# A halo of 32 columns instead of 8 in the x tile of a fused attention, channel mix and MLP kernel

## Chip, cores and metric

One core of a Trainium2 chip runs the kernel. The metric is the time of one execution on the device in microseconds, the median of several runs; lower is better.

## What is computed

Three layers follow each other on a batch of 4 sequences of 3072 tokens with 256 features, in float32:

```python
scores = (1.0 / S) * np.matmul(z, z.transpose(0, 2, 1))        # z: (4, 3072, 64)
x = u * np.matmul(np.maximum(scores, 0.0) ** 2, v)             # attention, gated by u

x_prev = x shifted by one token, zeros first
xk = mu_k * x + (1.0 - mu_k) * x_prev
xr = mu_r * x + (1.0 - mu_r) * x_prev
k = np.maximum(xk @ w_k, 0.0)                                  # w_k: (256, 1024)
x = 1.0 / (1.0 + np.exp(-(xr @ w_r))) * (k * k @ w_v)          # w_v: (1024, 256)

r = np.maximum(x.reshape(B * S, 256) @ w_in, 0.0)              # w_in: (256, 2048)
out = r * r @ w_out                                            # w_out: (2048, 256)
```

## The kernel before

Features lie on the 128 partitions and tokens along the free dimension, in blocks of T = 512 tokens; there are 24 blocks, and two neighbours make a pair (12 pairs). Every float32 operand is split into a high part and a rest, and each product is three matmuls: high by high, high by the weights' rest, rest by high. All matmuls have 512 moving columns.

Three stages use TensorE one behind the other. **Attention** makes scores from zz, keeps their squares in ahi and alo, and multiplies with vhl (L459); its matmuls have 64 rows, and two of them run at a time in the two halves of the array. The **channel mix** begins with the first two blocks done plainly (the plain stage: operands in mixed and hhi and hlo, weights in wk, wr and wv), and then takes the other 11 pairs with Winograd's form of a 2 by 2 matrix product (the mixed stage, since the work of three units is woven into each other by a planner in mix_groups). The **second MLP** takes all 12 pairs, numbered 0 to 11, in the same form.

In the Winograd form a pair is worked off in groups: 4 groups a pair in the mixed stage, 8 in the second MLP. A group is 7 products (product, L871, three matmuls each) between which the 8 down projections of the group before it are woven (down2, L887 to L889, three matmuls each): p0, d0, p1, d1, ..., p6, d6, d7, so 45 matmuls. In the mixed stage groups 1 and 2 of a pair have two gate sums of six matmuls besides (L219): 57. TensorE works this order off as written. Group i of the second MLP takes its up weights from win[i // 2]; the down projection of group i takes its weights from wout[i // 2], and runs during group i + 1.

The moving operands of products are made from a pair's x tile, x2. `pair_tile` makes it with HALO columns in front of each of its two halves of features; the last of them holds the token before the pair (`load_pair`, `before_x` read from column HALO - 1, L733 loads and L740 reads), and `pair_x` is the view without the halo. VectorE forms differences in place and in d13 (L833 to L837), then the operands are split: in the mixed stage and for pair 0 of the second MLP into unit tiles (L90, L764: u0 to u6, and two more, units 7 and 8, in a tile called mixed), later into the tiles ops0 (even pairs) and ops1 (odd pairs), whose names in the trace are b and d. The results of a product are summed on VectorE (L903), and go through relu, square and split on ScalarE and VectorE into hhi and hlo (L908, L912, L90, L920), the moving operands of the down projections.

Where the tiles lie in a partition follows from the order in which pools are made, since each side is a stack. On the left side x2 is the last tile but a few of its pool, and all that is made after it lies behind it. In bytes, with the remainder by 256 in brackets:

| tile | place before | role |
|---|---|---|
| vhl | 26880 and up (0) | weights in attention |
| zz | 76544 and up (0) | weights and moving, attention |
| ahi, alo | 105216 to 137984 (0) | moving, attention |
| hhi, hlo | 39168 to 63744 (0) | moving, down projections |
| x2 | 63744 to 72000 (0) | source of the operands |
| sig0, sig1, d13 | 72000, 74048, 76096 (64) | gates, differences |
| win0, wout0, win1, wout1 | 80192, 94528, 102720, 117056 (64) | weights, second MLP |
| u0 to u6 | 125248 to 153920 (64) | moving, products |
| ops0 (b, d of even pairs), in the place of u0 to u6 from pair 1 on | 125248 to 153920 (64) | moving, products |
| ops1 (b, d of odd pairs), ws, wk, wv, wr, mixed | 155392 and up (0) | moving and weights |
| win2, wout2, win3, wout3 | 184064, 198400, 206592, 220928 (0) | weights, second MLP |

All blocks of weights within a tile step by 512 bytes, all moving operands by 2048.

Of the kernel before, what the change touches and what calls it, by code (L numbers as in the profile page):

```python
# [23 lines left out]
def tile_relu2_attention__rwkv_channel_mix__relu2_mlp(  # L24
# [691 lines left out]

    unit = {}

    HALO = 8

    def pair_tile(s):
        x2_raw[s] = hp.tile([P, ND, HALO + 2 * T], F32, tag="x2", name="x2")
        return x2_raw[s]

    def pair_x(s):
        return x2_raw[s][:, :, HALO:].rearrange("x c (b t) -> x c b t", b=2)

    def load_pair(s):
# [3 lines left out]
        if t0:  # L732
            nc.sync.dma_start(out=t[:, :, HALO - 1:], in_=src[:, :, t0 - 1:t0 + 2 * T])  # L733
        else:
            nc.vector.memset(t[:, :, HALO - 1:HALO], 0.0)
            nc.sync.dma_start(out=t[:, :, HALO:], in_=src[:, :, 0:2 * T])

    def before_x(s, b, c, m):
        t0 = HALO - 1 + b * T
        nc.scalar.activation(out=m, in_=x2_raw[s][:, c, t0:t0 + T], func=AF.Copy, scale=om[:, 0, c:c + 1])  # L740
# [822 lines left out]
```

## Time and profile before

| | |
|---|---|
| median of 3 runs | 2495.2 us (2493.74 to 2495.23) |
| the profiled execution | 2495.45 us |
| its span, first to last instruction | 2493.6 us |
| TensorE busy | 2483.6 us (100%) |
| VectorE busy | 2104.8 us (84%) |
| ScalarE busy | 1823.0 us (73%) |
| granted clock of TensorE | 1.000 |
| chain of work that ended last | TensorE 94% of the span |

The span holds the kernel's instructions; some 1.9 us of the execution lie around it. Busy times are unions of an engine's instructions. The ends of matmuls are modelled, and each is shown longer than the distance to the next one's start, so for TensorE the starts are to be read.

### The profile page before, as it was taken

The page shows a single profiled execution, that of the slowest core. Times are in us where ns is not written, and L with a number is a line of the kernel's source. Part 1 is how long each engine was busy: PE and PEld are TensorE (multiplying, and loading weights), DVE is VectorE, ACT ScalarE, POOL GpSimd, SP SyncE. Part 2 cuts the span into 40 slices and gives each one's busy share as a digit, 9 for nine tenths or more (in the row PEclk, how much of TensorE's full clock was granted, in tenths as well). Part 3 has the DMA queues.
Part 4 walks back from the last instruction along what each step waited for, and adds up shares of the span by engine and source line. Part 5 has one row for each costly group of instructions (what it writes and reads, how often), then busy time and mean ns, then how long its engine had stood idle before and what let it go on. Part 6 is the DMA issues. An engine that isn't in the chain of part 4 may idle for free.

```text
span 2493.6 us, 39375 instructions
## 1 busy us (share of the span) xinstructions
PE 2483.6 (100%) x14721; PEld 2057.5 (83%) x14721; DVE 2104.8 (84%) x3499; ACT 1823.0 (73%) x3240; POOL 0.7 (0%) x6
## 2 busy tenths in 40 slices
PE   9999999999999999999999999999999999999999
PEld 7888898889988998888888888888888888888887
DVE  8898999889899889999999988777777777777776
ACT  8867977887698668888888877666666666666665
POOL 0000000000000000000000000000000000000000
PEclk9999999999999999999999999999999999999999
DMA  6676777767767752232132120110011001100100
GB/s 208 191 222 184 217 197 197 206 197 204 216 178 208 200 164 93 72 106 81 65 113 85 51 73 30 34 34 18 17 34 34 18 18 34 34 17 18 34 17 17
DMA packets 309439, 257.92 MB, mean 103 GB/s; under 512 B 205312, under 2 KB 224768, under 8 KB 306176
## 3 DMA queue, kind: packets, MB, share of 16 engines
q1 hardware_dynamic: 307136, 254.89, 34.8%
q8 instruction: 115, 1.88, 0.3%
q10 hardware_dynamic: 2112, 0.52, 0.1%
q14 instruction: 76, 0.62, 0.1%
HBM read 149.45 MB, written 105.91 MB: 102 GB/s over the span
## 4 chain that ended last, share of the span: by engine, by line
PE 94%; ACT 3%; DVE 1%; issue 1%; DMA 0%; SPq 0%; DVEq 0%
PE v L459 27%; PE ups L871 27%; PE v L887 10%; PE v L889 10%; PE v L888 10%; PE sps L421 4%; PE ups L219 4%; ACT a L382 1%; ACT a L425 1%; DVE alo L435 0%; DVE turn L362 0%; ACT vhl L328 0%; DMA mixed<-turned 0%; PE v L240 0%; PE v L238 0%
## 5 line engine op out<-in xcount | busy, mean ns | idle before, releaser
L459 PE MATMUL v<-ahi,vhl 64*128 64x512 f32 x4592 | 675.8, 387 | 0.0
L459 PEld LDWEIGHTS v<-ahi,vhl 64*128 64x128 f32 x4592 | 487.8, 184 | 69.6 <-ACT rest L469 3.7
L908 ACT ACTIVATE s<-s 128x512 f32<-128x512 f32 x288 | 181.0, 629 | 342.1 <-DVE s L903 342.1
L459 PE MATMUL v<-alo,vhl 64*128 64x512 f32 x2296 | 418.0, 386 | 0.2 <-DVE alo L435 0.2
L887 PE MATMUL v<-hhi,wout 128*128 128x512 f32 x768 | 303.2, 395 | 0.0
L889 PE MATMUL v<-hlo,wout 128*128 128x512 f32 x768 | 302.3, 394 | 0.0
L888 PE MATMUL v<-hhi,wout 128*128 128x512 f32 x768 | 301.6, 393 | 0.0
L871 PE MATMUL ups<-d,win 128*128 128x512 f32 x1056 | 301.1, 393 | 0.0
L459 PEld LDWEIGHTS v<-alo,vhl 64*128 64x128 f32 x2296 | 261.7, 184 | 34.0 <-DVE alo L435 0.6
L920 DVE TENSOR_TENSOR hlo<-s,hhi 128x512 fp32r<-128x512 f32 x384 | 264.5, 689 | 14.5 <-ACT hhi L90 1.0
L903 DVE TENSOR_TENSOR s<-ups,su 128x512 f32<-128x512 f32 x192 | 131.8, 687 | 126.9 <-PE ups L871 126.9
L871 PEld LDWEIGHTS ups<-d,win 128*128 128x128 f32 x1056 | 198.2, 188 | 45.7
L912 ACT ACTIVATE s<-s 128x512 f32<-128x512 f32 x384 | 231.3, 628 | 6.1
L871 PE MATMUL ups<-b,win 128*128 128x512 f32 x792 | 225.9, 393 | 0.0
L435 DVE TENSOR_TENSOR alo<-a,ahi 128x512 fp32r<-128x512 f32 x334 | 219.6, 661 | 0.0
L425 ACT ACTIVATE a<-a 128x512 f32<-128x512 f32 x334 | 211.4, 633 | 10.3
L362 DVE STREAM_TRANSPOSE turn<-a 128x512 f32<-128x512 f32 x240 | 206.7, 861 | 13.2 <-ACT a L425 11.9
L382 ACT ACTIVATE a<-sps 128x512 f32<-128x512 f32 x335 | 197.7, 590 | 20.2 <-PE sps L421 15.3
L871 PEld LDWEIGHTS ups<-b,win 128*128 128x128 f32 x792 | 148.7, 188 | 34.2
L889 PEld LDWEIGHTS v<-hlo,wout 128*128 128x128 f32 x768 | 144.1, 188 | 34.4
L887 PEld LDWEIGHTS v<-hhi,wout 128*128 128x128 f32 x768 | 144.2, 188 | 33.5
L888 PEld LDWEIGHTS v<-hhi,wout 128*128 128x128 f32 x768 | 144.3, 188 | 33.4
(201 smaller groups left out, 4284.5 us busy)
## 6 DMA issues: line engine op xcount, KB each, us to landing
turned<-turn SPq DMA_DIRECT2D x60, 1024.0 KB, 5.0
mixed<-turned SPq DMA_DIRECT2D x220, 256.0 KB, 5.1
u<-in_u_dram SPq DMA_DIRECT2D x192, 64.0 KB, 3.6
xT<-uT SPq DMA_DIRECT2D x48, 256.0 KB, 2.3
x2d<-sig SPq DMA_DIRECT2D x48, 256.0 KB, 2.1
x<-x2d SPq DMA_DIRECT2D x12, 1024.0 KB, 4.8
out_dram<-y SPq DMA_DIRECT2D x94, 128.0 KB, 2.3
raw<-in_v_dram SPq DMA_DIRECT2D x23, 512.0 KB, 5.2
```

What stands on the lines that cost most here:

```text
L362: nc.vector.transpose(t[:, :, :, c, :], a.rearrange("x (m r q) -> x q m r" if s else "x (m q r) -> x q m r", m=G, q=R))
L382: nc.scalar.activation(out=a, in_=ps, func=AF.Relu, scale=1.0 / S)
L425: nc.scalar.activation(out=a, in_=a, func=AF.Square)
L435: finish(lambda: nc.vector.tensor_tensor(out=lo, in0=a, in1=hi, op=ALU.subtract))
L459: nc.tensor.matmul(acc[n, d][i], lhsT=vt[rows, k % 2, c, ds_], rhs=at[s][k // 2][rows], start=first and k == 0, stop=last and k == 2)
L871: nc.tensor.matmul(ps, lhsT=weight(g, h, w), rhs=ops[g[0], j][y], start=first and m == 0, stop=m == 2, skip_group_check=not first)
L887: nc.tensor.matmul(acc[p, b][d], lhsT=w[:, 0, c, ds_], rhs=hi, start=first, stop=False)
L888: nc.tensor.matmul(acc[p, b][d], lhsT=w[:, 1, c, ds_], rhs=hi, start=False, stop=False)
L889: nc.tensor.matmul(acc[p, b][d], lhsT=w[:, 0, c, ds_], rhs=lo, start=False, stop=last)
L908: nc.scalar.activation(out=tmp[g, c], in_=banks[g, 0] if c == "11" else tmp[g, c], func=AF.Relu, scale=1.0 if g[0] < NPAIR else HS)
L912: nc.scalar.activation(out=tmp[g, c], in_=tmp[g, c], func=AF.Square)
L920: nc.vector.tensor_tensor(out=lo, in0=tmp.pop((g, c)), in1=hi, op=ALU.subtract)
```

## The change

`HALO` becomes 32. Each half of x2 gets 24 more columns in front, 192 bytes a partition in all, and the tiles made behind it on the left side move by as much. The halo's last column still holds the token before the pair. `prep_x2` reads x12 and x21 through a view whose step is HALO + T, which becomes 544 columns; it names the same elements.

```diff
     unit = {}
 
-    HALO = 8
+    HALO = 32
 
     def pair_tile(s):
         x2_raw[s] = hp.tile([P, ND, HALO + 2 * T], F32, tag="x2", name="x2")
```

## Rows read from the trace of the kernel before

**Rows 1.** The page, part 1: engine, busy us, share of the span, instructions.

```profile
PE 2483.6 (100%) x14721; PEld 2057.5 (83%) x14721; DVE 2104.8 (84%) x3499; ACT 1823.0 (73%) x3240; POOL 0.7 (0%) x6
```

**Rows 2.** Waits of TensorE, whole span: total us, times, longest; first and last of five.

```profile
PE sps L421 <- ACT a L382: 1.3, 3, 0.5
...
PE v L459 <- DVE alo L435: 0.2, 1, 0.2
```

**Rows 3.** Plain, mixed, second MLP: length; busy us (instructions) PE PEld DVE ACT POOL; clock; DMA.

```profile
919.59:962.93 43.34, 43.34 (x192) 35.86 (x191) 39.43 (x71) 35.38 (x62) 0.00 (x0) 1.00 0.43 151
962.93:1482.19 519.26, 519.26 (x2245) 421.34 (x2244) 485.50 (x823) 432.14 (x777) 0.00 (x0) 1.00 0.23 79
1482.19:2486.85 1004.67, 1004.67 (x4344) 815.14 (x4342) 750.83 (x1210) 652.00 (x1164) 0.00 (x0) 1.00 0.09 26
```

**Rows 4.** TensorE in order of time: first products of groups in pairs 1, 2, 11.

```profile
1576.22 0.86 PE L871 MATMUL ups<-b,win 128*128 128x512 f32 x3
1586.72 0.86 PE L871 MATMUL ups<-b,win 128*128 128x512 f32 x3
...
1607.72 0.85 PE L871 MATMUL ups<-b,win 128*128 128x512 f32 x3
1618.17 0.86 PE L871 MATMUL ups<-b,win 128*128 128x512 f32 x3
1628.40 0.84 PE L871 MATMUL ups<-b,win 128*128 128x512 f32 x3
1638.60 0.84 PE L871 MATMUL ups<-b,win 128*128 128x512 f32 x3
1648.80 0.85 PE L871 MATMUL ups<-b,win 128*128 128x512 f32 x3
...
1711.46 0.85 PE L871 MATMUL ups<-b,win 128*128 128x512 f32 x3
1721.92 0.86 PE L871 MATMUL ups<-b,win 128*128 128x512 f32 x3
1732.39 0.86 PE L871 MATMUL ups<-b,win 128*128 128x512 f32 x3
...
2451.24 0.86 PE L871 MATMUL ups<-b,win 128*128 128x512 f32 x3
2461.47 0.84 PE L871 MATMUL ups<-b,win 128*128 128x512 f32 x3
```

**Rows 5.** The same view, consecutive matmuls: mixed stage, then group 7 of pair 1.

```profile
1067.71 0.86 PE L871 MATMUL ups<-u,wk 128*128 128x512 f32 x3
1068.40 0.40 PE L887 MATMUL v<-hhi,wv 128*128 128x512 f32 x1
1068.64 0.39 PE L888 MATMUL v<-hhi,wv 128*128 128x512 f32 x1
...
1069.10 0.40 PE L871 MATMUL ups<-u,wse 128*128 128x512 f32 x1
...
1639.96 0.84 PE L871 MATMUL ups<-d,win 128*128 128x512 f32 x3
```

**Rows 6.** Waits in the mixed stage (962.93 to 1482.19): total us, times, longest.

```profile
ACT st L908 <- PE ups L871: 30.6, 20, 2.9
...
DVE st L903 <- PE ups L871: 12.7, 28, 1.1
```

**Rows 7.** Groups by line and shape: busy us, mean ns; idle us before, releaser.

```profile
L740 ACT ACTIVATE st<-x,om 128x512 f32<-128x512 f32 x44 | 31.0, 716 | 0.2 <-DMA x<-xT 0.2
...
L764 DVE TENSOR_TENSOR u<-x,u 128x512 fp32r<-128x512 f32 x47 | 31.6, 682 | 0.4 <-ACT u L90 0.3
...
L764 DVE TENSOR_TENSOR mixed<-x,mixed 128x512 fp32r<-128x512 f32 x13 | 8.9, 682 | 0.0
```

**Rows 8.** The page, part 6: DMA issues, count, KB each, us to landing.

```profile
x<-x2d SPq DMA_DIRECT2D x12, 1024.0 KB, 4.8
```

**Rows 9.** A stretch of attention: length; PE busy us (instructions), clock, DMA.

```profile
500.00:600.00 100.00, 100.00 (x883) 1.00 0.66 194
```

## The prediction

> **What bounds the kernel now.** The page's first part comes first: TensorE is busy for 2483.6 of 2493.6 us [rows 1]. Busy time alone proves little, since the ends of matmuls are modelled, so the second view is who waited for whom on TensorE: five entries, 3.7 us together, the longest a wait of scores for ScalarE and the shortest 0.2 us [rows 2]. All of them are waits of attention or of the prologue. Behind attention TensorE waits for nothing that the view can show, so the end of the kernel is a number of matmuls times the distance from one start to the next. That distance is what has to be read.
>
> The third view is the table by stage [rows 3]. I cut it at matmul starts. The plain stage (all operands at multiples of 256 bytes) has 191 starts in 43.34 us: 226.9 ns each. The mixed stage has 44 groups, 22 of 45 and 22 of 57 matmuls, 2244 in all, in 519.26 us: 231.4 ns each. The second MLP has 96 groups of 45 and 24 closing matmuls; 4343 starts lie in 1004.67 us: 231.3 ns each. The granted clock is 1.00, the 2.4 GHz level, in all three. So from the first Winograd product on each matmul takes about 4.5 ns longer than in the plain stage, with the same 512 columns, the same type and no wait.
>
> The fourth view is the order of time on TensorE, at the first product of groups of the second MLP [rows 4]. Groups do the same 45 matmuls; they differ in where the operands lie. In pair 2, group 6 (first product at 1711.46) takes 10.46 us and group 7 10.47 us; the products' operands are in ops0, 64 bytes past a multiple of 256, the weights in win3, wout2 and wout3 at multiples. In pair 1, group 1 (1576.22 to 1586.72) takes 10.50 us with operands in ops1 at multiples, and weights in win0 and wout0 64 bytes past. Group 4 (1607.72) has aligned products, but projects group 3's hidden tiles down with wout1, 64 bytes past: 10.45 us. Groups 5, 6 and 7 are the only ones with every operand at a multiple of 256: 10.23, 10.20 and 10.20 us. Pair 11, the last, repeats it: its group 5 takes 10.23 us again. Groups 6 and 7 carry the same side work in pair 1 as in pair 2, so that isn't the difference: the addresses are. 10.20 us over 45 is 226.7 ns, the distance of the plain stage.
>
> The same view at a finer grain [rows 5] shows where it sits: in the mixed stage the step from the first L887 behind the products of u (u at +64, wk and wv at multiples) to L888 is 0.24 us, and six matmuls take 1069.10 - 1067.71 = 1.39 us; the first six of group 7 in pair 1, all aligned, take 1639.96 - 1638.60 = 1.36 [rows 4, 5].
>
> **The change part by part.** *What moves.* The x2 tile grows from 2 x 1032 x 4 = 8256 bytes a partition (32 x 256 + 64) to 2 x 1056 x 4 = 8448 (33 x 256). What stands behind it on the left side moves by 192 bytes, from +64 to +0: sig, d13, win0, wout0, win1, wout1, the units u0 to u6, and ops0. No instruction, order, wait or count changes; the side still ends (at 154112) before the right side's tiles (155392), and each moved tile still covers parts of the same tiles of attention, so the waits for their release are the same. Attention itself isn't touched.
>
> *Second MLP.* Every operand of every matmul then lies as in groups 5 to 7. 4343 starts at 226.7 ns are 984.6 us instead of 1004.67: **20.1 us less**.
>
> *Mixed stage.* The u operands move to the residue of the unit tiles 7 and 8 and of wk, wv, wr. I price it at the plain stage's 226.9 ns: 2244 x 226.9 = 509.2 us instead of 519.26: **10.1 us less**, as long as VectorE keeps up. It is busy for 485.50 of the 519.26 us [rows 3], 93%; of 509.2 it would be 95%. What hides it is its idle time, 33.8 us in this stage, of which its longest wait, for products, makes 12.7 us; ScalarE waits 30.6 us for products at one line [rows 6]. TensorE asks for 10.1 us of that. If the cover failed, TensorE would wait for the hidden tiles, and the most that can be given back is the 10.1 us. In the second MLP VectorE has 750.83 us of work in 984.6: no bound, and the groups at 10.20 us show it.
>
> *Engines.* VectorE and ScalarE read and write moved tiles too. VectorE's split of an operand takes 682 ns into u (at +64) and 682 ns into a unit at a multiple [rows 7]. I take nothing, from 1 ns less to 1 ns more an instruction by the rounding of these rows, all of it beside TensorE's work.
>
> *DMA.* 23 loads write x2, whose rows begin at +32 and +64 (x itself), afterwards at +128 and +0. Such a load takes 4.8 us [rows 8], and its first reader in the mixed stage, L740, waited 0.2 us for all of them together [rows 7]. A gain or a loss within it isn't seen by the end; with the cover gone, a load would cost its excess, tenths of a microsecond each, 23 times. I take nothing.
>
> *Tail.* What follows the last matmul is unchanged, and so is all ahead of the mixed stage.
>
> *Sum.* 2495.45 us of the profiled execution (span 2493.6 and 1.85 around it) less 20.1 and 10.1 is 2465.25; the median of the runs lies 0.25 lower: **2465.0 us**, 1.2% less. Next in line then is the distance of 226.7 ns itself, in every stage.
>
> **The rivals.** *A, slower: the residue that counts is of more than 256.* The tiles that are good today are all odd multiples of 256 (hi, lo, wv, win2, win3, ops1: remainder 256 by 512); the moved tiles become even multiples (win0 at 80384, remainder 0). If what matters is that moving operand and weights agree modulo 512 or more, the change only turns a difference of 64 into one of 256. Against it: within win and wout the blocks of weights step by 512 bytes, and groups 6 and 7 show no step. For it: no row of this trace has a difference of 256. It decides above 231.3 ns a matmul. With the dearest group of rows 4, 10.50 us or 233.3 ns for each of the 6587 starts, it would be 6587 x 2.0 = 13 us slower: 2508 us. Chance 0.07.
>
> *B, no change: not the address but the region or the company.* Today's slow operands all lie between 80192 and 153920, so "shifted" and "in the middle" are the same tiles. Against it: attention's ahi and alo are moving operands, and zz is both, at multiples of 256 in that same region, and a stretch of 100 us holds 883 half-array matmuls, one more or less at its edges, two of which run at a time [rows 9]: 100 / 441 = 226.8 ns for two, the good distance. For it: those are half-array matmuls of 64 rows. It gives 2495 us. The Trainium skill, in SBUF — State Buffer, section Specifications (TRN2), gives a cacheline of 16 bytes; +64 is a multiple of 16, and by that alone the two places would read equally fast and the time would stay at 2495 us. The trace disagrees with that reading: 10.20 against 10.46 us for the same group. Chance 0.05.
>
> *C, part is given back.* VectorE, with 5% of idle time left in the mixed stage, lets TensorE wait at some groups, or a few matmuls keep some ns: 2466 to 2490 us, about 2475 if the mixed stage gains nothing. For it: in that stage VectorE is the nearest engine; against: TensorE hasn't one wait there today. Chance 0.08.
>
> *The forecast*, 2465 us: 0.80.
>
> **How the numbers follow.** The forecast's own bounds: 0.2 ns a matmul either way is 1.3 us, a run-to-run spread of 1.5 us, and the mixed stage's 10.1 us as the price of lost cover on the upper side. Low 2461, high 2476: this holds the forecast nearly whole (0.78) and half of C (0.04). Faster by over 0.2%, 5 us, about what a measurement of this kernel can tell from no change: 0.80 + 0.08 = 0.88. Within: B, 0.05. Slower: A, 0.07.
>
> **What would show it.** Right, if in the profile after all groups of the second MLP take 10.20 us in even and odd pairs alike, the stage from the first product with win to the last matmul some 985 us, the mixed stage some 509, the plain stage 43.3 as now, and TensorE's waits behind attention stay empty. Even pairs at 10.46 would mean B; even pairs changed but not at 10.20, or odd groups 5 to 7 fast while 1 to 4 stay at 10.50, would mean A; entries "PE <- DVE" in the mixed stage would mean C. The forecast is wrong if the distance between matmul starts depends on something that the moved tiles share with their neighbours besides the last 8 bits of their address.

## The result and the profile after

The changed kernel takes 2464.0 us (2463.4 to 2465.6, 4 runs) against 2494.5 of the kernel before: a ratio of 0.988, 95% interval 0.986 to 0.990. The profiled execution took 2465.6 us, its span is 2463.8. The forecast was 2465.0, and its range 2461 to 2476 holds the time.

The table by stage of the changed kernel (plain, mixed, second MLP; length, busy us and instructions of PE, PEld, DVE, ACT, POOL, then clock, DMA share, GB/s). The second MLP is taken from the start of its first matmul to the start of its last:

```profile
920.64:963.98 43.34, 43.34 (x192) 35.85 (x191) 39.46 (x71) 35.40 (x62) 0.00 (x0) 1.00 0.43 151
963.98:1472.62 508.64, 508.64 (x2245) 421.17 (x2244) 484.81 (x823) 431.21 (x777) 0.00 (x0) 1.00 0.24 81
1472.62:2457.19 984.57, 984.57 (x4344) 814.90 (x4343) 749.51 (x1210) 652.16 (x1164) 0.00 (x0) 1.00 0.09 27
```

The row of the second MLP in [rows 3] ends at 2486.85, the start of the last matmul but one, so it holds 4342 starts and not 4343 (the count of instructions in a row takes in those that only reach into its stretch). Taken to the start of the last matmul, the kernel before has (length, busy us and instructions of PE, clock, DMA share, GB/s):

```profile
1482.19:2487.08 1004.89, 1004.89 (x4344) 1.00 0.09 26
```

The plain stage is what it was, 43.34 us. The mixed stage lost 519.26 - 508.64 = 10.6 us, the second MLP 1004.89 - 984.57 = 20.3. Both now run at 226.7 ns a matmul (508.64 / 2244, 984.57 / 4343), at the same clock level as before. The span is shorter by 29.8 us, not by 30.9, because the first Winograd product starts at 963.98 instead of 962.93, 1.05 us later, and what follows the last matmul's start took 6.61 us instead of 6.53.

TensorE in order of time, the first products of the groups that [rows 4] shows (pair 1, groups 1, 2, 4, 5, 6, then pair 2, groups 6 and 7; start us, us, line, tiles):

```profile
1564.42 0.84 PE L871 MATMUL ups<-b,win 128*128 128x512 f32 x3
1574.62 0.84 PE L871 MATMUL ups<-b,win 128*128 128x512 f32 x3
...
1595.02 0.84 PE L871 MATMUL ups<-b,win 128*128 128x512 f32 x3
1605.22 0.84 PE L871 MATMUL ups<-b,win 128*128 128x512 f32 x3
1615.42 0.84 PE L871 MATMUL ups<-b,win 128*128 128x512 f32 x3
...
1697.05 0.84 PE L871 MATMUL ups<-b,win 128*128 128x512 f32 x3
1707.25 0.84 PE L871 MATMUL ups<-b,win 128*128 128x512 f32 x3
```

Group 1 took 10.50 us and takes 10.20; group 4, 10.45 and now 10.20; group 6 of pair 2, 10.46 and now 10.20. There is no difference left between even and odd pairs.

Two entries of TensorE's waits over the whole span, the first and the last of the list (total us, times, longest), then one of ScalarE's and one of VectorE's in the mixed stage:

```profile
PE sps L421 <- ACT a L382: 2.1, 4, 0.7
PE v L459 <- DVE alo L435: 0.2, 1, 0.2
```

```profile
ACT st L908 <- PE ups L871: 26.1, 18, 2.7
DVE st L903 <- PE ups L871: 9.8, 24, 0.8
```

As in [rows 2], nothing behind attention stands among TensorE's waits. The time that TensorE saved in the mixed stage came out of the others' idle time: VectorE's fell from 33.8 to 508.64 - 484.81 = 23.8 us, and of the waits for products 30.6 became 26.1 and 12.7 became 9.8 us [rows 6].

### The profile page after: what moved, and what is told of

Read it like the earlier page. It is cut to its first block, busy times and chain, and to the rows that moved or that the text cites. A ratio compares the mean times of both kernels' runs of the same rounds, so it can differ in the third digit from the quotient of the medians.

```text
span 2463.8 us, 39375 instructions
## 1 busy us (share of the span) xinstructions
PE 2452.8 (100%) x14721; PEld 2073.9 (84%) x14721; DVE 2102.7 (85%) x3499; ACT 1821.8 (74%) x3240; POOL 0.7 (0%) x6
## 4 chain that ended last, share of the span: by engine, by line
PE 94%; ACT 2%; DVE 1%; issue 1%; SPq 1%; DMA 1%; DVEq 0%; ACTq 0%
PE v L459 27%; PE ups L871 27%; PE v L887 10%; PE v L889 10%; PE v L888 10%; PE sps L421 4%; PE ups L219 4%; ACT a L382 1%; ACT a L425 1%; SPq L274 0%; DVE alo L435 0%; ACT vhl L328 0%; DMA mixed<-turned 0%; DMA zn<-in_z_dram 0%; SPq L376 0%
## 5 line engine op out<-in xcount | busy, mean ns | idle before, releaser
L459 PEld LDWEIGHTS v<-ahi,vhl 64*128 64x128 f32 x4592 | 497.1, 184 | 60.0 <-ACT rest L469 3.7
L887 PE MATMUL v<-hhi,wout 128*128 128x512 f32 x768 | 298.8, 389 | 0.0
L888 PE MATMUL v<-hhi,wout 128*128 128x512 f32 x768 | 298.8, 389 | 0.0
L871 PEld LDWEIGHTS ups<-b,win 128*128 128x128 f32 x792 | 148.7, 188 | 30.9
```

The source lines that it names most:

```text
L459: nc.tensor.matmul(acc[n, d][i], lhsT=vt[rows, k % 2, c, ds_], rhs=at[s][k // 2][rows], start=first and k == 0, stop=last and k == 2)
L871: nc.tensor.matmul(ps, lhsT=weight(g, h, w), rhs=ops[g[0], j][y], start=first and m == 0, stop=m == 2, skip_group_check=not first)
L887: nc.tensor.matmul(acc[p, b][d], lhsT=w[:, 0, c, ds_], rhs=hi, start=first, stop=False)
L888: nc.tensor.matmul(acc[p, b][d], lhsT=w[:, 1, c, ds_], rhs=hi, start=False, stop=False)
```

## The experiments

All but the first are single profiled executions, to be read by their stages. In each table below the rows are the mixed stage and the second MLP, taken as above: stretch, length, PE busy us (instructions), clock, DMA share, GB/s. Wherever its tiles lie alike, the mixed stage repeats to a hundredth of a microsecond (508.64) and the second MLP to 0.2 (984.41 in e10 to 984.62), so differences of half a microsecond can be read.

**The halo undone, the places kept (e1).** In `pair_tile`, behind the first x2:

```diff
-    HALO = 32
+    HALO = 8
...
+        if s == PLAIN:
+            hp.tile([P, 48], F32, name="pad")
```

> The halo stays at 8 columns and an unused tile of 192 bytes stands right behind x2, so that all tiles further on lie where the changed kernel has them. Theory 1 (places): only the places of what lies behind x2 count, so the time is that of the changed kernel, 2464 us, with every group of the second MLP at 10.20 us. Rival (the halo itself: x2's rows, its loads and its readers lie better): the time stays near that of the kernel before, 2494 us, or comes out between the two.

2463.0 us (2462.8 to 2463.9, 4 runs; ratio to before 0.987, 0.986 to 0.989).

```profile
961.15:1469.79 508.64, 508.64 (x2245) 1.00 0.24 81
1469.79:2454.41 984.62, 984.62 (x4344) 1.00 0.09 27
```

Both stages are those of the changed kernel. The wider halo is worth nothing by itself, neither for its loads nor for its readers; an unused tile does as much.

**Weights alone at +64 (e2).**

```diff
+        w3.tile([P, 16], F32, name="pad")
         for q in range(2):
             w_tiles(w3, q)
+        w3.tile([P, 48], F32, name="pad2")
```

> As the changed kernel, with win0, wout0, win1 and wout1 alone put back to 64 bytes past a multiple of 256 (a 64-byte tile in front of them, 192 bytes behind). Theory 1: weights count by themselves. By the odd pairs of the kernel before (moving operands aligned, these weights at +64) groups 1 to 3 take 10.50 us, group 0 and group 4 10.45, group 5 10.23 and groups 6 and 7 10.20, now in even and odd pairs alike: 1.42 us a pair over 8 x 10.20, 12 pairs, 17 us; 2481 us, the mixed stage at 508.6. Rival (only the moving operand counts): 2464 us, all groups at 10.20.

2482.4 us, against 2481 expected.

```profile
963.93:1472.57 508.64, 508.64 (x2245) 1.00 0.24 81
1472.57:2473.94 1001.37, 1001.37 (x4344) 1.00 0.09 26
```

First products of groups 6 and 7 of pair 1 and of groups 1 and 2 of pair 2:

```profile
1618.20 0.84 PE L871 MATMUL ups<-b,win 128*128 128x512 f32 x3
1628.40 0.84 PE L871 MATMUL ups<-b,win 128*128 128x512 f32 x3
...
1649.03 0.86 PE L871 MATMUL ups<-b,win 128*128 128x512 f32 x3
1659.53 0.86 PE L871 MATMUL ups<-b,win 128*128 128x512 f32 x3
```

10.20 us where win3 and wout2 serve, 10.50 where win0 and wout0 do, in an even pair too, whose operands are now aligned. In groups 1 to 3 all weights lie at +64 and all moving operands at +0: 10.50 us over 45 is 233.3 ns, on average 6.7 more a matmul, with no change of place from one moving operand to the next or from one weight block to the next. So the quarrel is between moving operands and weights.

**Moving operands alone at +64 (e3).**

```diff
         for q in range(2):
             w_tiles(w3, q)
+        w3.tile([P, 16], F32, name="pad")
```

> As the changed kernel, with u0 to u6 and ops0 alone put back to 64 bytes past a multiple of 256. Theory 1: moving operands count by themselves: the mixed stage is back at some 519 us (10.6 more), all eight groups of even pairs are at some 10.46 us as groups 4 to 7 were before (6 x 8 x 0.26 = 12.6 us), odd pairs but pair 0's neighbour stay at 10.20: 2487 us. Rival (only the weights count): 2464 us.

2486.5 us, against 2487 expected.

```profile
961.32:1480.58 519.26, 519.26 (x2245) 1.00 0.23 79
1480.58:2478.06 997.48, 997.48 (x4344) 1.00 0.09 26
```

The mixed stage is back at the 519.26 us of [rows 3]: there it was u alone. In the second MLP, group 2 of pair 1 (ops1) and group 6 of pair 2 (ops0) begin and end so:

```profile
1584.75 0.84 PE L871 MATMUL ups<-b,win 128*128 128x512 f32 x3
1594.95 0.84 PE L871 MATMUL ups<-b,win 128*128 128x512 f32 x3
...
1708.76 0.86 PE L871 MATMUL ups<-b,win 128*128 128x512 f32 x3
1719.23 0.86 PE L871 MATMUL ups<-b,win 128*128 128x512 f32 x3
```

10.20 against 10.47 us.

**The right side at +64 instead of the left (e4).** The tile "even" at the right edge has 40 columns instead of 56.

> As the changed kernel, with everything on the right side moved by 64 bytes instead (the tile at that side's edge has 40 columns instead of 56): wk, wv, wr, mixed, ws, ops1, win2, wout2, win3, wout3 are at +64, all of the left side at multiples of 256. Theory 1: they become slow as the left ones were: mixed stage near 233.4 ns a matmul, 524 us (15 more); in the second MLP groups 4 to 7 of even pairs near 10.50 and all of odd pairs near 10.45 (about 19 us more); together near 2499 us. Rival (only tiles in the middle of the partition, 80192 to 153920, are sensitive): 2464 us.

2497.6 us, against 2499 expected. The first row is the plain stage:

```profile
918.02:962.07 44.05, 44.05 (x192) 1.00 0.44 149
962.07:1484.15 522.08, 522.08 (x2245) 1.00 0.23 79
1484.15:2489.19 1005.04, 1005.04 (x4344) 1.00 0.09 26
```

Tiles that had always been fast become slow, and the tiles in the middle of the partition, now at multiples, don't help. The plain stage pays for the first time: hhi and hlo at +0, wv at +64. Where in the partition a tile lies doesn't matter; that is the end of rival B.

**Everything at +64 (e5).** The small tile behind the first x tile has 24 columns instead of 8, and the one at the right edge 40 instead of 56.

> As the changed kernel, with everything on both sides moved by 64 bytes (the small tile behind the first x tile has 24 columns instead of 8, the one at the right edge 40 instead of 56): every moving operand and every weight tile lies 64 bytes past a multiple of 256, hi, lo, vhl, zz, ahi and alo too. Theory 1a (each place counts by itself): no matmul is free; with 64 against 64 at 229 to 233 ns in the kernels so far, at least 4 ns for each of the 6587 starts of the mixed stage and the second MLP, so 2464 + 26 = 2490 us or more, and up to some 2510 if attention pays as well. Theory 1b (what counts is that moving operands and weights that follow each other lie alike modulo 256): 2464 us.

2466.6 us, 1.0 more than the profiled execution of the changed kernel; that lies behind the last matmul's start, where 7.6 us pass instead of 6.6.

```profile
963.99:1472.62 508.64, 508.64 (x2245) 1.00 0.24 81
1472.62:2457.24 984.62, 984.62 (x4344) 1.00 0.10 27
```

No operand of these two stages' matmuls is at a multiple of 256, and both take what they take in the changed kernel. Theory 1a, the one on which the forecast was built, falls: no place is good or bad by itself. Theory 1b stands: what TensorE streams and what it loads must lie alike.

**Other distances (e6, e7, e8).** HALO = 16, 36 and 12: the tiles behind x2 lie at +128, +32 and +96.

> A halo of 16 columns: the tiles behind x2 lie 128 bytes past a multiple of 256. If the step that counts is 256 bytes: slow, even pairs and odd groups 1 to 4 well over 10.20 us, in all 2480 to 2510 us. If it is 128 bytes: 2464 us, all groups at 10.20.

> A halo of 36 columns: the tiles behind x2 lie 32 bytes past a multiple of 256. If any offset costs the same as 64 bytes: 2494 us. If the cost grows with the offset: some 15 us over the changed kernel, 2479 us. If places 32 bytes off read as fast (a unit of 32 bytes): 2464 us.

> A halo of 12 columns: the tiles behind x2 lie 96 bytes past a multiple of 256. If the step is 256 and any offset costs the same: 2494 us. If the cost grows with the offset: more than the kernel before, 2500 to 2515 us. If the step is 128 and the distance to the nearest multiple counts (32 bytes here): as with 36 columns.

2491.4, 2491.2 and 2492.4 us. In this order:

```profile
962.60:1480.22 517.62, 517.62 (x2245) 1.00 0.24 79
1480.22:2483.01 1002.79, 1002.79 (x4344) 1.00 0.09 26
```

```profile
962.05:1479.66 517.62, 517.62 (x2245) 1.00 0.23 79
1479.66:2482.83 1003.16, 1003.16 (x4344) 1.00 0.09 26
```

```profile
961.31:1477.82 516.51, 516.51 (x2245) 1.00 0.23 79
1477.82:2484.03 1006.21, 1006.21 (x4344) 1.00 0.09 26
```

All three cost nearly what 64 bytes cost (519.26 and 1004.89): 27 to 30 us over the changed kernel's two stages together, where the kernel before is 30.9 over them. The cost isn't proportional to the distance, 32 bytes aren't tolerated, and 128 aren't a step. A distance of 256 is: in the changed kernel u, ops0, win0 and wout0 are even multiples of 256, and hi, lo, wk, wv, win2 and ops1 odd ones, and their mixture runs at 226.7 ns.

**Each matmul's own operands alike, the place changing every three matmuls (e9).** Layout of win0, win1 (+64), wout0, wout1 (+0), u and ops0 (+64):

```diff
+        if q < 2:
+            pool.tile([P, 16], F32, name=f"pad{q}")
         win[q] = pool.tile([P, 2, 2, 7, P], F32R, name=f"win{q}")
+        if q < 2:
+            pool.tile([P, 48], F32, name=f"rest{q}")
         wout[q] = pool.tile([P, 2, G, D], F32R, name=f"wout{q}")
```

and 16 columns more ahead of the units.

> As the changed kernel, but u0 to u6, ops0, win0 and win1 lie 64 bytes past a multiple of 256 and wout0 and wout1 at one. In groups 0 to 3 of even pairs each matmul's moving operand and weights then lie alike (products 64 with 64, down projections 0 with 0), but every three matmuls the place changes. If a matmul's own two operands are what counts: these groups take 10.20 us. If what is loaded for the next matmul meets what this one streams: 2 of 6 matmuls pay some 6.7 ns, 10.30 us. If all that runs must lie alike: 10.43 us as in the kernel before. Elsewhere the operands differ as before: mixed stage 519 us, groups 4 to 7 of even pairs 10.46 us; groups 0 to 3 of odd pairs (products 0 with 64, down projections 0 with 0) between 10.20 and 10.50. Together 2485 to 2492 us.

2491.9 us.

```profile
962.01:1481.27 519.26, 519.26 (x2245) 1.00 0.23 79
1481.27:2483.49 1002.21, 1002.21 (x4344) 1.00 0.09 26
```

Group 2 of pair 2, where each matmul's two operands agree (L875 is the product here; the three matmuls of a down projection stand between the first two rows):

```profile
1668.32 0.85 PE L875 MATMUL ups<-b,win 128*128 128x512 f32 x3
...
1669.71 0.86 PE L875 MATMUL ups<-d,win 128*128 128x512 f32 x3
...
1678.76 0.85 PE L875 MATMUL ups<-b,win 128*128 128x512 f32 x3
```

Six matmuls take 1.39 us as in [rows 5], the group 10.44: what the third answer forecast. That a matmul's own two operands agree gains nothing as long as the place changes every three matmuls. Since a slower distance outlasts its cause by several matmuls (last section), this run does not exclude the second answer with its cost spread over the neighbours; what is shown is that for the short distance a whole stretch must lie alike.

**Attention's moving operands at +64 (e10).**

```diff
             io = st.enter_context(tc.tile_pool(name="io", bufs=2))
+            io.tile([P, 16], F32, name="pad", bufs=1)
```

> As the changed kernel, with a 64-byte tile in front of attention's io pool: ahi and alo (moving operands of L459) lie at +64, the weights vhl and both operands of the scores (zz) at multiples of 256; all behind attention is unchanged. If half-array matmuls pay like the others (6.7 ns for each of some 3444 pairs of L459): attention takes 23 us more, 942 us instead of 919, and the whole 2487 us; VectorE, busy for 90% of that stage, hides none of it since TensorE is the bound. If the 64-row form doesn't pay: 2464 us.

2478.1 us. Two stretches of attention and the mixed stage:

```profile
300.00:400.00 100.00, 100.00 (x867) 1.00 0.75 197
500.00:600.00 100.00, 99.76 (x859) 1.00 0.68 192
976.66:1485.30 508.64, 508.64 (x2245) 1.00 0.24 81
```

From 300 to 400 us TensorE is busy throughout in both kernels and starts 867 half-array matmuls instead of 881 in the kernel before: 230.7 ns for two instead of 227.0, 3.7 more. From 500 to 600 it is 859 instead of the 883 of [rows 9], 232.8 ns instead of 226.5; that is the dearest of the stretches of 100 us between 100 and 900, and TensorE waits 0.24 us in it. Over the whole of attention the first Winograd product starts 976.66 - 963.98 = 12.7 us later, some 3.7 ns for each of 3444 pairs, not the 6.7 expected (runs with the same attention differ by up to 2.8 us there, 961.15 to 963.98). So the 64-row form pays as well, at about half the price that was taken from the full matmuls. With vhl and zz at +64 too (e5), the stretch from 500 to 600 holds 883 again.

## Why the prediction was right, point by point

**The bound.** Right. TensorE had no wait behind attention and has none now, and the time saved is matmuls times distance: 6587 starts by 4.7 ns less (10.6 + 20.3 us).

**What moves.** Right, and e1 sharpens it: the halo is only a way of moving the rest.

**Second MLP, 20.1 us.** Measured 20.3. The working took 4343 starts for a row that holds 4342; over like stretches it gives 1004.89 - 984.6 = 20.3 us. Groups 5 to 7 of pair 1 were a sample of the changed kernel within the kernel before. The groups right behind a pair's change, with index 1, take 10.20 to 10.23 us (1646.02 to 1656.25 us in pair 2) instead of 10.20. They lose it in the two to six matmuls from the first down projection of the new pair on (last section). A likely reason is a wait of a few ns for the eviction of the pair before (L927), too short for the view of waits; that was not tried.

**Mixed stage, 10.1 us.** Measured 10.6. The term was priced a little too dear: the plain stage's 226.9 ns held a slow beginning of its own (its first nine starts in that stretch are 224 to 236 ns apart), and from there on it runs at 226.7, as the mixed stage now does. VectorE kept up at 484.81 of 508.64 us, 95%, as worked out; rival C didn't come.

**Engines and DMA, nothing.** The lines that answer to [rows 7] and [rows 8] in the changed kernel:

```profile
L740 ACT ACTIVATE st<-x,om 128x512 f32<-128x512 f32 x44 | 30.9, 717 | 0.4 <-DMA x<-xT 0.3
L764 DVE TENSOR_TENSOR u<-x,u 128x512 fp32r<-128x512 f32 x47 | 31.8, 687 | 0.4 <-ACT u L90 0.3
L764 DVE TENSOR_TENSOR mixed<-x,mixed 128x512 fp32r<-128x512 f32 x13 | 8.9, 687 | 0.0
```

```profile
x<-x2d SPq DMA_DIRECT2D x12, 1024.0 KB, 4.7
```

The split takes 687 instead of 682 ns into the moved u and, as much, into the unmoved mixed. These 5 ns lie outside the 1 ns that was allowed, but the new place isn't their cause, since mixed shows them too. The load takes 4.7 instead of 4.8 us. None of it is on the path.

**What failed.** One step of the reasoning, which did the sum no harm: "Groups 5, 6 and 7 are the only ones with every operand at a multiple of 256". That is true, but I took the multiple for the cause. They are also the only groups in which all operands lie alike, and the trace of before can't tell the two apart, because every tile that isn't at +64 is at +0. Rival A named the right kind of rule, agreement instead of place, and had its step wrong: agreement is asked for modulo 256, not 512 or more, so even and odd multiples may be mixed. Had its step been 512, the same reading of the same rows would have forecast 30 us that don't come: rival A put that case 13 us slower, and by e6 to e8, where every difference that costs at all costs about the same, it would have been near no change. That the step is 256 was luck as far as the rows of before go. The chance of 0.07 was small: that blocks of weights step by 512 bytes speaks against a step of more than 512, and no row spoke against 512 itself.

**Rival B** fell with the changed kernel itself (the tiles still lie in the middle) and with e4. The sentence of the Trainium skill that stood beside it (SBUF — State Buffer, Specifications (TRN2), the 16-byte cacheline) describes no difference between +0 and +64. By e5 there is none for a tile by itself; the trace disagrees only where two operands of TensorE differ.

## What to carry to other kernels

Where TensorE runs back to back, read the distance between matmul starts, not its busy time, and look in the same trace for stretches in which the same work runs faster: they price a change of layout before it is made. Let all tiles that TensorE reads, weights and moving operands, start at the same remainder by 256 bytes; it is the agreement that counts, in a whole stretch, not the remainder. The runs show this for float32 operands, with 512 columns. A small unused tile behind the one with the odd size does it, and a halo's width need not be touched.

## What the runs showed of the hardware beyond that

- With float32 operands of 512 columns, the distance between starts is 226.7 ns when all agree. When all weights lie 64 bytes off all moving operands it is 233.3 ns (e2). Work on VectorE and ScalarE is an unlikely cause: in e2 group 1 takes 10.50 us in each of the 12 pairs, whatever else is done beside it.
- A slower distance outlasts its cause. In e2, group 5 of pair 1 has operands that all agree; its first six matmuls still take 1.39 us, and only the next six 1.36:

```profile
1607.97 0.86 PE L871 MATMUL ups<-b,win 128*128 128x512 f32 x3
...
1609.36 0.84 PE L871 MATMUL ups<-d,win 128*128 128x512 f32 x3
...
1610.72 0.84 PE L871 MATMUL ups<-d,win 128*128 128x512 f32 x3
```

How long it lasts differs. In e3, behind the last product from ops0 of pair 2, sixes of agreeing matmuls take 1.39, 1.38 and then 1.36 us. And it doesn't need operands that differ: in the changed kernel, where all agree, group 1 of pair 2 begins with sixes of 1.38 and 1.37 us before it comes to 1.36:

```profile
1646.02 0.84 PE L871 MATMUL ups<-b,win 128*128 128x512 f32 x3
...
1647.40 0.85 PE L871 MATMUL ups<-d,win 128*128 128x512 f32 x3
...
1648.77 0.84 PE L871 MATMUL ups<-d,win 128*128 128x512 f32 x3
...
1650.13 0.84 PE L871 MATMUL ups<-d,win 128*128 128x512 f32 x3
```

So after a disturbance the distance settles over some matmuls, up to about ten here. That fits e9, where agreement in pairs of operands isn't enough. Why the distance grows when moving operands and weights start at different remainders, and why it settles slowly, no run here shows; it stays open. So does whether other types, or fewer columns, pay the same.
